# Seven half-products for eight in three pairs of pg and two of po, and ph to po in one planned order

## The chip, the cores and the metric

The kernel runs on 1 core of one Trainium2 chip. The metric is the device time of one execution in microseconds (us). The engines that matter are TensorE (PE; its weight loads are PEld), VectorE (DVE), ScalarE (ACT), GpSimd (POOL) and the DMA queue that SyncE (SP) issues.

## What is computed

An attention block and two feed-forward blocks, in float32:

```python
# q, k, v: (2, 12, 448, 64), causal attention in float32
scores = (q @ k.T) / 8, masked above the diagonal; attn = exp(scores - max); attn = attn / (sum + 1e-9)
x = (attn @ v) as (896 tokens, 768)
h = max(max(x @ w1, x @ w2), x @ w3)        # w1, w2, w3: (768, 768)
y = h @ wo                                  # (768, 768)
p = y @ w_in                                # (768, 2048)
g = where(p > 0, p, exp(min(p, 0)) - 1)
out = g @ w_out                             # (2048, 768)
```

The four weight matrices arrive as 64-bit floats; the kernel decodes their words into float32 itself.

## The kernel before

**Layout.** Everything is held transposed: features lie on the 128 partitions, tokens along the free dimension, 448 tokens for each of the two batches b. x, h and y are 6 chunks of 128 features for each b, g is 16. Each such tile is [128, 2, 448]: a high part that the fast matmul type (fp32r) holds exactly, and the rest, a low part. A weight block [128, n, 128] is split likewise into `hi` and `lo`. One product of a chunk is three matmuls of 448 columns: hi with high, hi with low, lo with high (`products`, L250, L251, L253).

**Stages.** Attention (12 head pairs), then ph (h: three matrices, 6 output blocks f, both b), py (y, 6 blocks), pg (16 blocks), po (6 blocks over 16 chunks, its weights in parts of 6, 5 and 5 chunks). A block of py or pg is 2 x 6 x 3 = 36 matmuls, a block of po 2 x 16 x 3 = 96.

**A weight's steps** (`less_steps` and `load_steps`): an SP transfer of 768 KB into one of two `w_raw` buffers, four steps on VectorE (L209, L212, L214, and after a ScalarE step at L216 the merge at L218), the high part on ScalarE (L236), the low part on VectorE (L224). There are two `w_raw`, two `w_f` and three pairs of hi/lo buffers.

**Seven products for eight in ph.** `unit(n, f1, f2)` computes two output blocks of one matrix for both b. It halves K (chunks 0 to 2 and 3 to 5), so that 2 batches x 2 halves x 2 blocks would be eight half-products of 3 chunks, 9 matmuls each, and it uses a scheme that needs seven. The price: sums of x over batches and halves, made once (`add_totals`, then `whole` splits each into high and low); two differences of weight blocks, "13" and "24" (`less_of`, L751), each split into high and low (`split`, L734, L224); three copies of a partial product into another PSUM bank, so that several results can go on from it (`seed`, L791), one product kept in SBUF (`out5`, L803) and added to two results (`both` in `leave`, L641). Five such units run, for blocks 1 to 4 of ph.

**Order.** Attention is ordered by one `Plan`, ph by a second one, `late_plan`: each task has engines with costs, tasks it comes after, buffers it takes and gives, and a rank; `order` picks greedily, and the result is each engine's program order (`manual_schedule`). TensorE's products are chained in one line (`on_pe`, 203 ns for each matmul). `late_plan` ends with the first two weights of py. py, pg and po are plain loops after it; there the order of each engine is that of the program text, and tiles are waited for as they are used.

**py, pg, po.** py's two results are split into y by ScalarE (L847) and VectorE (L156). pg's result goes through the ELU: two ScalarE steps (L862, L863), one VectorE step that joins (L866), a ScalarE high part (L868) and a VectorE low part (L156). po's results are copied out (L885) and stored. PSUM's eight banks go round.

Of the kernel before, what the change touches and what calls it, by code (L numbers as in the profile page):

```python
# [8 lines left out]
F32 = mybir.dt.float32  # L9
# [31 lines left out]
UNITS = ((1, 2), (3, 4))  # L41
FIRST = NK - 1
# [13 lines left out]
LOAD = (("DMA", 2300), ("DVE", 560), ("DVE", 356), ("DVE", 555), ("ACT", 937), ("DVE", 958))  # L56

# [75 lines left out]
def fused_kernel(ctx: ExitStack, tc: tile.TileContext, qk, v, w1, w2, w3, wo, wi2, wo2, outT):  # L133
# [7 lines left out]
    ident = const.tile([128, 128], F32, name="ident")  # L141
    make_identity(nc, ident)
    def causal(name, w, rows):

        m = const.tile([128, w], F32, name=name)
        nc.gpsimd.memset(m, 0.0)
        for at in range(0, 128, rows):
            own = m[at:at + rows, w - rows:]
            nc.gpsimd.affine_select(
                out=own, in_=own, compare_op=ALU.is_ge, fill=NEG, base=0, pattern=[[-1, rows]], channel_multiplier=1)  # L150
        return m

    mask, mask_r = causal("mask", FULL, C), causal("mask_r", S, R)

    def sub(eng, out, a, b):
        return eng.tensor_tensor(out=out, in0=a, in1=b.bitcast(F32), op=ALU.subtract)  # L156

    lift = const.tile([128, 1], F32, name="lift")
# [97 lines left out]
    y = [[None] * NK for _ in range(B)]  # L256

    with ExitStack() as s1:
        xp = s1.enter_context(tc.tile_pool(name="xp", bufs=2 * NK))
        bp = s1.enter_context(tc.tile_pool(name="bp", bufs=2))  # L260

        def keep_best(best, ps, n):
            if n == 0:
                nc.scalar.copy(best, ps)
            else:
                nc.vector.tensor_tensor(out=best, in0=ps, in1=best, op=ALU.max)

        AHEAD = [(f, n) for f in range(3) for n in range(3)][:AHEADS]
        tots = ExitStack()
        totp = tots.enter_context(tc.tile_pool(name="totp", bufs=4 * HALF, side="right"))  # L270
        totals = {(q, c): totp.tile([128, S], F32, tag="t", name=f"t{q}_{c}") for q in range(4) for c in range(HALF)}
        ahead, bests = {}, {}

        with ExitStack() as s2:
            raws = s2.enter_context(tc.tile_pool(name="raws", bufs=3))
            ap = s2.enter_context(tc.tile_pool(name="ap", bufs=PAIRS))
            thp = s2.enter_context(tc.tile_pool(name="thp", bufs=THS))
            small = s2.enter_context(tc.tile_pool(name="small", bufs=PAIRS))
            ps_s = s2.enter_context(tc.tile_pool(name="ps_s", bufs=SBANKS, space=PSUM))
            ps_t = s2.enter_context(tc.tile_pool(name="ps_t", bufs=6 - SBANKS, space=PSUM))  # L280
            plan = Plan(
                {"qk": QKS, "v": 3, "s": SBANKS, "pt": 6 - SBANKS, "m": 2, "pr": PAIRS, "th": THS, "raw": 2, "f": 2})
            engines = {"ACT": nc.scalar, "DVE": nc.vector, "POOL": nc.gpsimd}

            def copy(eng, out, a):
                (nc.scalar.copy if eng == "ACT" else engines[eng].tensor_copy)(out, a)

            ones, ones_row = (nc.const_aps.tensor(1.0, [128, w], BF16) for w in (128, 512))

            def warm(eng, n):  # L290

                idle = ps_m.tile([128, 512], F32, tag="m", name="idle")
                for _ in range(n):
                    nc.tensor.matmul(idle, ones, ones_row, start=True, stop=True)

            plan.add(warm, (8,), {"PE": 4200}, 0, takes=["m"], gives=["m"])

            SCORES = ((2, 0), (NB,), (1,))  # L300
            COLS = {(2, 0): 0, (2, 1): 1, (0, 0): 2, (0, 1): 3, (1, 0): 4, (1, 1): 5, (NB, None): 6}
            PARTS = ((0, 6), (6, 7))

            TURNS = (((0, 0, (0, 1, 2)),), ((1, 0, (0, 1, 2)),), ((0, 1, (1, 2)), (1, 1, (1, 2))),
                     ((0, 2, (2,)), (1, 2, (2,))), tuple((None, c, (NB,)) for c in range(NB + 1)))


            th_r = [thp.tile([C, 2, R], F32, name=f"th_r{n}", bufs=1) for n in range(THS)]
            for t in th_r:
                nc.gpsimd.memset(t, 0.0)  # L310

            us, xs_done, shares = {}, {}, []

            def heads(i):
                return (None,) if i == NB else (1, 0)

            def pair(p):

                u = us[p] = {}
                odd = p % 2  # L320

                def load(eng, part):
                    if "qk" not in u:
                        u["qk"] = raws.tile([128, 2, S], F32, tag="qk", name=f"qk{p}", bufs=QKS)
                    nc.sync.dma_start(u["qk"][:, :, part], qk[p][:, :, part])

                def load_v(eng):
                    u["v"] = raws.tile([C, 2, NB + 1, D], F32, tag="v", name=f"v{p}")
                    nc.sync.dma_start(u["v"], v[p])

                def scores(eng, g):

                    for e in (p, p + 1)[:1 + (g == 1)]:
                        us[e]["s", g] = [ps_s.tile([C, 512], F32, tag="s", name=f"s{e}_{g}_{j}") for j in range(2 - (g == 1))]
                    at = 0
                    for i in SCORES[g]:
                        w = min(C * (i + 1), S)
                        for e in (p, p + 1)[:1 + (i == NB)]:
                            for j in range(2):
                                own, to = slice(D * j, D * (j + 1)), j ^ (e % 2)  # L340
                                s = us[e]["s", g]
                                out = s[0][D * to:D * (to + 1), :w] if i == NB else s[j][:, at:at + w]
                                nc.tensor.matmul(  # L343
                                    out, us[e]["qk"][own, 0, C * i:w], us[e]["qk"][own, 1, :w], start=True, stop=True,
                                    skip_group_check=True)
                        at += w

                def least(eng, g, j):

                    if "nmx" not in u:  # L350
                        u["nmx"] = small.tile([C, len(COLS)], F32, tag="nmx", name=f"nmx{p}")
                        u["l"] = small.tile([C, len(COLS)], F32, tag="l", name=f"l{p}")
                    at = 0
                    for i in SCORES[g]:
                        w, n = min(C * (i + 1), S), COLS[i, j]
                        pr = u["pr", j, i] = ap.tile([C, w], F32, tag=f"pr{i}_{j}", name=f"pr{p}_{j}_{i}")
                        nc.vector.tensor_tensor_reduce(  # L357
                            out=pr, in0=u["s", g][j or 0][:, at:at + w],
                            in1=mask_r if i == NB else mask[:, FULL - w:], scale=-0.125, scalar=3.0e38,
                            op0=ALU.add, op1=ALU.min, accum_out=u["nmx"][:, n:n + 1],  # L360
                        )
                        at += w

                def exps(eng, g, j):
                    for i in SCORES[g]:
                        pr, n = u["pr", j, i], COLS[i, j]
                        nc.scalar.activation(  # L367
                            pr, pr, AF.Exp, bias=u["nmx"][:, n:n + 1], scale=-1.0, accum_out=u["l"][:, n:n + 1])

                def guard(eng, a, b):  # L370
                    engines[eng].tensor_scalar_add(u["l"][:, a:b], u["l"][:, a:b], 1e-9)

                def inverse(eng, a, b):
                    if "r" not in u:
                        u["r"] = small.tile([C, len(COLS)], F32, tag="r", name=f"r{p}")
                    nc.vector.reciprocal(u["r"][:, a:b], u["l"][:, a:b])  # L376

                def normalise(eng, i, j):
                    n = COLS[i, j]
                    engines[eng].tensor_scalar(  # L380
                        out=u["pr", j, i], in0=u["pr", j, i], scalar1=u["r"][:, n:n + 1], scalar2=1.0,
                        op0=ALU.mult, op1=ALU.mult)

                def turn(eng, t):
                    pt = u["pt", t] = ps_t.tile([128, 512], F32, tag="pt", name=f"pt{p}_{t}")
                    at = 0
                    for j, c, blocks in TURNS[t]:
# [5 lines left out]
                def turned(eng, t):  # L393

                    if "th" not in u:
                        u["th"] = thp.tile([C, NB, 2, S], F32, tag="th", name=f"th{p}")
                        u["th_r"] = th_r[p % THS]
# [529 lines left out]
```

## Time and profile before

| | |
|---|---|
| time, median of 3 runs | 483.97 us (482.69 to 485.89) |
| the profiled execution | 483.52 us, its span 481.70 us |
| TensorE busy | 474.9 us, 99% of the span, 2555 matmuls |
| VectorE busy | 351.8 us, 73%, 729 instructions |
| ScalarE busy | 254.6 us, 53%, 522 instructions |
| GpSimd busy | 47.7 us, 10% |
| transfers | 55.88 MB, mean 116 GB/s |
| mean granted TensorE clock | 0.999 |

A share of busy time is an average over stages; the stages begin at about 95 (ph alone), 204.67 (py), 247.87 (pg) and 363.07 us (po). Matmuls are pipelined, so one matmul's own duration (362 ns) is longer than the distance between two.

### The profile page before, as it was taken

What the parts mean: (1) busy time and instruction counts of PE and PEld (TensorE: products, weight loads), DVE (VectorE), ACT (ScalarE), POOL (GpSimd) and SP (SyncE); (2) the same over time, 40 slices, a digit from 0 to 9 for tenths busy, and PEclk for the clock granted to TensorE, in tenths of its full rate; (3) what the DMA queues carried; (4) which work ended last, traced back from release to release, by engine and by line L of the source; (5) the groups of instructions that cost most, each with busy time, mean ns of one, the idle gap of its engine ahead of it and who ended that gap; (6) DMA issues with size and microseconds to landing.
All of it is one profiled execution on the core that took longest, in us unless ns stands there. A gap on an engine that the chain in (4) does not pass through costs nothing.

```text
span 481.7 us, 6957 instructions
## 1 busy us (share of the span) xinstructions
PE 474.9 (99%) x2555; PEld 416.6 (86%) x2555; DVE 351.8 (73%) x729; ACT 254.6 (53%) x522; POOL 47.7 (10%) x101
## 2 busy tenths in 40 slices
PE   8999999999999999999999999999999999999997
PEld 3556666799999999999999999999999999999996
DVE  4999999699999999788767787687676544545310
ACT  5999796464464665455336666666664323322200
POOL 3575443500000000000000000000000000000000
PEclk9999999999999999999999999999999999999999
DMA  6626413013433333234433233233234434244011
GB/s 198 222 85 201 149 46 152 1 67 131 138 132 123 132 130 134 65 132 153 175 131 121 77 132 120 78 131 116 64 117 120 141 127 151 78 144 147 0 39 38
DMA packets 13969, 55.88 MB, mean 116 GB/s; under 512 B 1520, under 2 KB 3568, under 8 KB 13936
## 3 DMA queue, kind: packets, MB, share of 16 engines
q1 hardware_dynamic: 13936, 55.45, 33.9%
q8 instruction: 20, 0.33, 0.3%
q14 instruction: 13, 0.11, 0.1%
HBM read 52.69 MB, written 2.75 MB: 115 GB/s over the span
## 4 chain that ended last, share of the span: by engine, by line
PE 92%; DVE 4%; DMA 1%; POOL 1%; SPq 0%; issue 0%; ACT 0%; DVEq 0%; ACTq 0%
PE pg L251 8%; PE po L251 8%; PE po L253 8%; PE pg L253 8%; PE po L250 8%; PE pg L250 8%; PE p L778 7%; PE ps L778 6%; PE ph L250 4%; PE ph L251 4%; PE ph L253 4%; PE pt L390 4%; PE s L343 4%; PE o L413 3%; PE py L251 3%; PE py L253 3%
## 5 line engine op out<-in xcount | busy, mean ns | idle before, releaser
L251 PE MATMUL pg<-y,hi_wi 128*128 128x448 f32 x192 | 69.6, 362 | 0.0
L251 PE MATMUL po<-g,hi_wo 128*128 128x448 f32 x192 | 69.6, 362 | 0.0
L250 PE MATMUL po<-g,hi_wo 128*128 128x448 f32 x192 | 69.6, 362 | 0.0
L250 PE MATMUL pg<-y,hi_wi 128*128 128x448 f32 x192 | 69.6, 362 | 0.0
L253 PE MATMUL po<-g,lo_wo 128*128 128x448 f32 x192 | 54.8, 362 | 0.0
L253 PE MATMUL pg<-y,lo_wi 128*128 128x448 f32 x192 | 54.0, 362 | 0.0
L216 ACT ACTIVATE f_wo<-f_wo,lift 128x768 uint32<-128x768 int16 (+1 forms) x24 | 21.2, 886 | 43.4 <-DVE f_wo L214 43.3
L236 ACT ACTIVATE hi_wo<-f_wo 128x768 fp32r<-128x768 f32 (+1 forms) x24 | 19.0, 793 | 42.8 <-PE po L251 35.9
L224 DVE SCALAR_TENSOR_TENSOR lo_wo<-f_wo,hi_wo 128x768 fp32r<-128x768 f32 (+1 forms) x24 | 21.3, 891 | 26.6 <-ACT hi_wo L236 26.4
L367 ACT ACTIVATE pr<-pr,nmx 128x384 f32<-128x384 f32 (+1 forms) x72 | 35.9, 502 | 5.8 <-DVE nmx L357 5.7
L250 PEld LDWEIGHTS po<-g,hi_wo 128*128 128x128 f32 x192 | 36.0, 188 | 2.4
L253 PEld LDWEIGHTS po<-g,lo_wo 128*128 128x128 f32 x192 | 36.0, 188 | 2.4
L250 PEld LDWEIGHTS pg<-y,hi_wi 128*128 128x128 f32 x192 | 36.0, 188 | 2.4
L251 PEld LDWEIGHTS pg<-y,hi_wi 128*128 128x128 f32 x192 | 36.0, 188 | 2.4
L253 PEld LDWEIGHTS pg<-y,lo_wi 128*128 128x128 f32 x192 | 36.0, 188 | 2.4
L251 PEld LDWEIGHTS po<-g,hi_wo 128*128 128x128 f32 x192 | 36.0, 188 | 2.4
L250 PE MATMUL ph<-x,hi_w 128*128 128x448 f32 x96 | 35.3, 368 | 0.2 <-DVE x L156 0.2
L218 DVE SCALAR_TENSOR_TENSOR f_wo<-raw_wo,f_wo 128x768 int32<-128x768 int32 (+1 forms) x24 | 21.3, 891 | 19.4 <-ACT f_wo L216 19.3
L251 PE MATMUL ph<-x,hi_w 128*128 128x448 f32 x96 | 34.8, 363 | 0.0
L357 DVE CUSTOM_DVE_ANT_0 pr<-s,mask 128x384 f32<-128x384 f32 (+1 forms) x72 | 26.7, 414 | 7.0 <-PE s L343 6.9
L380 POOL TENSOR_SCALAR pr<-pr,r 128x384 f32<-128x384 f32 (+2 forms) x57 | 30.2, 548 | 12.1 <-DVE r L376 6.6
L253 PE MATMUL ph<-x,lo_w 128*128 128x448 f32 x96 | 30.0, 363 | 0.0
(143 smaller groups left out, 995.1 us busy)
## 6 DMA issues: line engine op xcount, KB each, us to landing
raw_w<-in_w SPq DMA_DIRECT2D x18, 768.0 KB, 4.6
raw_wi<-in_wi SPq DMA_DIRECT2D x16, 768.0 KB, 4.3
raw_wo<-in_wo SPq DMA_DIRECT2D x12, 768.0 KB, 4.5
raw_wo<-in_wo SPq DMA_DIRECT2D x12, 640.0 KB, 4.0
qk<-in_qk SPq DMA_DIRECT2D x11, 448.0 KB, 4.8
v<-in_v SPq DMA_DIRECT2D x12, 256.0 KB, 2.9
out_t<-ot SPq DMA_DIRECT2D x12, 224.0 KB, 3.0
qk<-in_qk SPq DMA_DIRECT2D x1, 256.0 KB, 3.2
```

Of the source, the lines that this page charges most:

```text
L216: nc.scalar.activation(f.bitcast(U32), y, AF.Relu, bias=lift, scale=2.0 ** 19)
L218: nc.vector.scalar_tensor_tensor(out=f, in0=below, scalar=13, in1=f, op0=ALU.logical_shift_right, op1=ALU.bitwise_or)
L224: nc.vector.scalar_tensor_tensor(out=lo, in0=f, scalar=-1.0, in1=hi.bitcast(F32), op0=ALU.mult, op1=ALU.subtract)
L250: nc.tensor.matmul(ps, hi[:, c, :], xs[cc][:, 0, :], start=(cc == 0), stop=False)
L251: nc.tensor.matmul(ps, hi[:, c, :], xs[cc][:, 1, :], start=False, stop=False)
L253: nc.tensor.matmul(ps, lo[:, c, :], xs[cc][:, 0, :], start=False, stop=(cc == total - 1))
L343: nc.tensor.matmul(out, us[e]["qk"][own, 0, C * i:w], us[e]["qk"][own, 1, :w], start=True, stop=True, skip_group_check=True)
L357: nc.vector.tensor_tensor_reduce(out=pr, in0=u["s", g][j or 0][:, at:at + w], in1=mask_r if i == NB else mask[:, FULL - w:], scale=-0.125, ...
L367: nc.scalar.activation(pr, pr, AF.Exp, bias=u["nmx"][:, n:n + 1], scale=-1.0, accum_out=u["l"][:, n:n + 1])
L380: engines[eng].tensor_scalar(out=u["pr", j, i], in0=u["pr", j, i], scalar1=u["r"][:, n:n + 1], scalar2=1.0, op0=ALU.mult, op1=ALU.mult)
L390: nc.tensor.transpose(pt[:e - C * c, at:at + C], u["pr", j if j is None else j ^ odd, i][:, C * c:e], ident)
L778: nc.tensor.matmul(ps[0], wt[:, HALF * k + c], w[:, i, :], start=(new and c == m == 0), stop=(c == HALF - 1 and m == 2), skip_group_check= ...
```

## The change

1. `unit` is made general (weights, left operand, sums and what becomes of the results are handed in) and gets a `lean` form with fewer buffers: one for both weights (`ub`), one for difference "13" (`u13`), two for the split differences (`ul`); difference "24" is formed in place over the weight buffer, once the first weight has been split.
2. pg computes blocks (2, 3), (6, 7) and (10, 11) by lean units over y. Their sums, `y_sums`, are formed from py's PSUM results, a chunk c as soon as blocks c and c + 3 are there; for that py goes through its blocks in the order 0, 3, 1, 4, 2, 5.
3. po computes blocks (2, 3) and (4, 5) by lean units for chunks 0 to 5 of g (768 of 2048 features); chunks 6 to 15 follow as two parts for each block, on the same banks. The sums over g, `sums_g`, are formed in the first blocks of po: eight VectorE steps a chunk, then four splits.
4. py, pg and po become tasks of `late_plan`, which now orders ph to po as one list; its SLACK goes from 200 to 110 and its overlap for VectorE from 70 to 60.
5. Tiles are reused by stage: y takes x's tiles, g those of h, then fresh ones, then those of the sums; the ELU's and the sums' intermediates use the `best` buffers of ph. The masks and `ident` move into the attention stage's pool, and POOL's small memset of `lift` comes before them. The size reserved for software DMA descriptors goes to 1024.

The core of the diff, without the re-indentation:

```diff
+PY = (0, 3, 1, 4, 2, 5)
+PG_UNITS = (2,6,10,)
+PO_UNITS = (2,4,)
...
-        late_plan.OVER = {"DVE": 70, "ACT": 60}
-        late_plan.SLACK = 200
+    late_plan.OVER = {"DVE": 60, "ACT": 60}
+    late_plan.SLACK = 110
...
-        def unit(n, f1, f2):
+    def unit(name, src, lean, left, sums, leave, kind="p"):
...
+        u, ut, tk = ("ub", "u13", "ul") if lean else ("u", "ut", "t")
...
+        if lean:
+            def less_in(at_, ab):
+                def sub_(eng):
+                    fs["24"] = slots(slice(1, 3)).rearrange("p s (c f) -> p (s c) f", c=HALF)
+                    a, b = ab()
+                    nc.vector.tensor_tensor(out=fs["24"][:, at_], in0=a, in1=b, op=ALU.subtract)
+                return sub_
+            t2 = task(less_in(dn, lambda: (fs[1][:, dn], fs["13"][:, up_])), "DVE", 555, at, [t1])
+            t4 = task(less_in(up_, lambda: (fs[0][:, dn], fs["24"][:, dn])), "DVE", 555, at, [t2, ready[0]])
...
+    renewed = task(again, "-", 0, clock[0] - 1000, [line[0], *left_last], gives=["ub", "u13", "ul", "ul", "ot", "ot"])
...
+    def y_sums(c, banks):
...
+        t0 = step("21", 0, (p21,), [e21], ["best0"], [m(1, c)], "ACT")
+        t1 = step("s0", 1, ("21", p22), [t0, e22], ["best1"], [m(1, d)])
+        t3 = step("s2", 2, (p11, "21"), [t0, e11], ["best0"], [], op=ALU.subtract)
+        t2 = step("s1", 3, ("s0", p11), [t1, t3], ["best1"], [m(0, c)], op=ALU.subtract)
...
+        for q, t, tag in ((0, t2, "best1"), (2, t3, "best0"), (1, t4, "best1"), (3, t4, "best0")):
+            sums_y.whole(q, c, lambda q=q: sy_home(HALF * q + c), lambda q=q: tot[f"s{q}"], at + 500,
+                         [t, renewed], gives=[tag])
...
+    for f in PY:
+        y_block(f, py_banks if PG_UNITS else None)
+        if f >= HALF and PG_UNITS:
+            y_sums(f - HALF, py_banks)
...
+        if f in PG_UNITS:
+            def leave_g(k, b, ps, after, gives, at, more=None, frees=()):
+                if more is not None:
+                    after = [*after, added(ps, more, after, at, frees)]
+                elu(f + k, b, ps, after, at, gives)
+            unit(f"g{f}", [wi2[f], wi2[f + 1]], True, y, sums_y, leave_g, "pg")
+            f += 2
+            continue
...
+        groups = ((0, 1, 3, 4), (2, 5)) if f == 0 else (tuple(range(NK)),)
...
+    sums_g, begin = Sums(), clock[0]
...
+            for k, (q, a, b_, op) in enumerate((
+                    (3, (1, c, 0), (1, c, 1), ALU.add), (0, 3, (1, d, 0), ALU.add), (0, 0, (1, d, 1), ALU.add),
+                    (1, (0, c, 0), (0, c, 1), ALU.add), (2, 1, 3, ALU.subtract), (1, 0, 1, ALU.subtract),
+                    (3, (0, d, 0), 1, ALU.subtract), (3, 3, (0, d, 1), ALU.add))):
...
+                t = task(step, "DVE", 619, at, [t, line[0], *(g_done[b, e] for b in range(B) for e in (c, d))],
+                         takes=[f"best{q % 2}"] * (k in (0, 1, 3, 4)))
...
+            unit(f"o{f}", [wo2[f, :, :NK], wo2[f + 1, :, :NK]], True, g, sums_g, leave_o, "po")
+        for c0, n in ((0, 6), (6, 5), (11, 5))[pair:]:
+            for k in reversed(range(1 + pair)):
+                single = f + pair == NK - 1 and c0 + n == NF and k == 0
+                for bs, t in o_parts(f + k, outs[k], c0, n, c0 == 0, single, sum((ends.get((k, b), []) for b in range(B)), [])):
...
+    with tc.manual_schedule():
+        for fn, eng, args in late_plan.order({"DVE": 1200, "ACT": 1000}):
+            fn(eng, *args)
```

## Rows read from the trace of the kernel before

**Rows 1.** Busy time by stage; columns: stretch, its length, engines, PEclk, DMA, GB/s.

```profile
0.00:95.00 95.00, 91.64 (x640) 57.17 (x641) 80.82 (x281) 73.29 (x235) 47.66 (x101) 1.00 0.38 134
204.67:247.87 43.20, 43.20 (x218) 40.55 (x217) 33.48 (x55) 19.94 (x29) 0.00 (x0) 1.00 0.41 148
247.87:363.07 115.20, 115.20 (x578) 108.14 (x577) 83.83 (x142) 72.61 (x125) 0.00 (x0) 1.00 0.32 106
363.07:478.30 115.23, 115.20 (x577) 107.80 (x575) 50.53 (x82) 29.10 (x41) 0.00 (x0) 1.00 0.32 101
```

**Rows 2.** The chain that ended last: start, us, what.

```profile
141.67 5.40 PE p L778 x27
...
478.35 0.53 ACT ot L885
```

**Rows 3.** VectorE by line and form in ph's units, 141.67 to 204.67 us.

```profile
L218 DVE SCALAR_TENSOR_TENSOR b<-raw_w,b 128x768 int32<-128x768 int32 x8 | 7.6, 955 | 1.1 <-ACT b L216 0.9
L224 DVE SCALAR_TENSOR_TENSOR lo<-f,hi 128x768 fp32r<-128x768 f32 x8 | 7.5, 951 | 0.0
...
L751 DVE TENSOR_TENSOR f<-b,f 128x384 f32<-128x384 f32 x8 | 4.5, 558 | 0.2
L214 DVE TENSOR_TENSOR b<-b 128x768 int16<-128x768 int16 x7 | 3.9, 558 | 0.2
L751 DVE TENSOR_TENSOR f<-b 128x768 f32<-128x768 f32 x4 | 3.8, 958 | 0.1
...
L209 DVE TENSOR_SCALAR b<-raw_w 128x768 bf16<-128x768 bf16 x6 | 3.3, 554 | 0.0
...
L212 DVE TENSOR_SCALAR b<-b 128x768 int16<-128x768 int16 x7 | 2.5, 360 | 0.2
L641 DVE TENSOR_TENSOR p<-p,s 128x448 f32<-128x448 f32 x4 | 2.5, 628 | 0.1
...
L224 DVE SCALAR_TENSOR_TENSOR lo<-b,hi 128x384 fp32r<-128x384 f32 x4 | 2.2, 551 | 0.0
```

**Rows 4.** VectorE by line and form in pg, 247.87 to 363.07 us.

```profile
L156 DVE TENSOR_TENSOR g<-gf,g 128x448 fp32r<-128x448 f32 x30 | 17.3, 619 | 0.0
L866 DVE SCALAR_TENSOR_TENSOR gf<-e,pg 128x448 f32<-128x448 f32 x30 | 17.2, 614 | 0.0
L224 DVE SCALAR_TENSOR_TENSOR lo_wi<-f_wi,hi_wi 128x768 fp32r<-128x768 f32 x14 | 13.4, 958 | 13.1 <-ACT hi_wi L236 13.1
```

**Rows 5.** Busy time: two units of ph, two blocks of pg, two of po.

```profile
141.67:154.27 12.60, 12.60 (x65) 11.83 (x64) 11.93 (x19) 6.73 (x12) 0.00 (x0) 1.00 0.38 125
...
179.47:192.07 12.60, 12.60 (x65) 11.83 (x64) 12.18 (x21) 7.18 (x11) 0.00 (x0) 1.00 0.38 133
...
247.87:255.07 7.20, 7.20 (x38) 6.76 (x37) 4.37 (x7) 2.64 (x5) 0.00 (x0) 1.00 0.28 104
255.07:262.27 7.20, 7.20 (x38) 6.76 (x37) 5.35 (x9) 4.69 (x9) 0.00 (x0) 1.00 0.32 107
363.07:382.27 19.20, 19.20 (x98) 18.02 (x97) 11.51 (x20) 7.83 (x13) 0.00 (x0) 1.00 0.40 114
382.27:401.47 19.20, 19.20 (x98) 18.02 (x97) 9.90 (x17) 5.36 (x8) 0.00 (x0) 1.00 0.41 133
```

**Rows 6.** VectorE in order of time: start, us, what.

```profile
167.25 0.62 DVE L266 TENSOR_TENSOR best<-ps,best 128x448 f32<-128x448 f32 x1
167.79 0.61 DVE L156 TENSOR_TENSOR h<-best,h 128x448 fp32r<-128x448 f32 x1
```

**Rows 7.** VectorE in order of time, at the end of pg's second block.

```profile
261.02 0.96 DVE L218 SCALAR_TENSOR_TENSOR f_wi<-raw_wi,f_wi 128x768 int32<-128x768 int32 x1 [1.01 <-ACT f_wi L216]
```

**Rows 8.** ScalarE's copies between banks in ph's units, by line.

```profile
L791 ACT COPY ps<-p 128x448 f32<-128x448 f32 x15 | 7.8, 517 | 12.4 <-PE p L778 12.3
```

**Rows 9.** Who waited for whom in pg: us in total, times, longest.

```profile
ACT hi_wi L236 <- PE pg L251: 12.9, 13, 1.8
```

**Rows 10.** POOL in order of time: its first task behind the masks.

```profile
9.75 0.24 POOL L371 TENSOR_SCALAR l<-l 128x6 f32<-128x6 f32 x1 [6.56 <-ACT pr L367]
```

More of the change, by code (lines that the diff above doesn't have):

```diff
@@ L139, in fused_kernel @@
     ps_m = ctx.enter_context(tc.tile_pool(name="ps_m", bufs=2, space=PSUM))
[L141 to L153, printed above, removed]
     def sub(eng, out, a, b):
         return eng.tensor_tensor(out=out, in0=a, in1=b.bitcast(F32), op=ALU.subtract)
+    const.tile([128, 64], F32, name="place")
     lift = const.tile([128, 1], F32, name="lift")
@@ new lines, in fused_kernel, with on_pe, task, convert @@
+    clock, line = [0.0], [None]
+    PASS = 203.0
+    def on_pe(fn, n, after, **more):
+        t = late_plan.add(fn, (), {"PE": int(PASS * n)}, 0, [*after, line[0]], lead=clock[0], **more)
+        clock[0] += PASS * n
+        line[0] = t
+        return t
+    def task(fn, eng, cost, at, after, **more):
+        return late_plan.add(fn, (), {eng: cost}, 0, after, lead=at, **more)
+    LAST, LAST_5 = (("ACT", 848), ("DVE", 958)), (("ACT", 735), ("DVE", 825))
+    def convert(steps, costs, at, took, gave, begun=False):
+        got, t = [], None
+        def step(eng):
+            got[:] = [next(steps)]
+        for k, (eng, cost) in list(enumerate(costs))[begun:]:
+            t = task(step, eng, cost, at, [t], takes=took.get(k, ()), gives=gave.get(k, ()))
+        return got, t
@@ new lines, in finish, with high, low, standard @@
+    def finish(f, b, at, after):
+        def high(eng):
+            nc.scalar.copy(h[b][f][:, 0], best_of(f, b))
+        def low(eng):
+            sub(nc.vector, h[b][f][:, 1], best_of(f, b), h[b][f][:, 0])
+        t = task(high, "ACT", 570, at, [after])
+        hs_done[f, b] = task(low, "DVE", 617, at, [t], gives=[f"best{b}"])
+    def standard(n, f, over):
+        at, ps = clock[0], {b: [] for b in over}
+        parts, t = (([ahead[f, n]], None) if (f, n) in AHEAD else load(
+            (w1, w2, w3)[n][f], f"w{n}_{f}", at, begun.pop(n, None) if f == FIRST else None))
+        def product(eng):
+            for b in over:
+                ps[b].append(psum(f"ph{n}_{b}_{f}"))
+            products([ps[b][0] for b in over], *parts[0], [x[b] for b in over], 0, NK, NK)
+        t = on_pe(product, 18 * len(over), [t], takes=["m"] * len(over), gives=["w"])
+        for b in over:
+            leave(n, f, b, ps[b], [t], ["m"], clock[0] + 2000)
@@ new lines, in fused_kernel, with __init__, whole, high @@
+    class Sums:
+        def __init__(self):
+            self.parts, self.made = {}, {}
+        def whole(self, q, c, home, total, at, after, gives=()):
+            def high(eng):
+                self.parts[q, c] = home()
+                nc.scalar.copy(self.parts[q, c][:, 0], total())
+            def low(eng):
+                sub(nc.vector, self.parts[q, c][:, 1], total(), self.parts[q, c][:, 0])
+            t = task(high, "ACT", 570, at, after)
+            self.made[q, c] = task(low, "DVE", 617, at, [t], gives=gives)
@@ L637, in leave, with put, out @@
+    def put(f, b, ps, after, at, eng, gives, more=None, frees=()):
+        def out(eng_):
+            ot = pools["ot"].tile([128, S], F32, tag="ot", name=f"ot{f}_{b}")
+            rows = outT[128 * f:128 * (f + 1), S * b:S * (b + 1)]
             if more is not None:
[L639 to L645 removed]
@@ L830, in fused_kernel @@
-        opened = task(reopen, "-", 0, 0, list(made.values()))
-        for fs_ in UNITS:
-            for n in range(1 if fs_ == UNITS[0] else 0, 3):
-                unit(n, *fs_)
-        wos = [load(wo[f], f"wo_{f}", clock[0] + 7300 * f)[0] for f in range(2)]
-        with tc.manual_schedule():
-            for fn, eng, args in late_plan.order({"DVE": 1200, "ACT": 1000}):
-                fn(eng, *args)
-        up.close()
-        ctx.enter_context(tc.tile_pool(name="pad", bufs=1, side="right")).tile([128, 24], F32, name="pad")
@@ L871, in fused_kernel @@
[L871 to L886 removed]
+                nc.vector.tensor_tensor(out=ot, in0=ps[0], in1=more[0], op=ALU.add)
+            else:
+                (nc.scalar.copy if eng == "ACT" else nc.vector.tensor_copy)(ot, ps[0])
```

1077 lines of the change are left out of this document (592 added, 485 removed).

## The prediction

> **What bounds the kernel now.** I read the busy times by stage first. TensorE is busy for all of the 43.20 us of py, the 115.20 us of pg and the 115.20 us of po; the only idle time worth a name is 3.36 us in the attention stage (95.00 less 91.64) and the 3.40 us between the end of po at 478.30 and the end of the span at 481.70 [rows 1]. In the chain of waits the second half of the span is nothing but matmuls, 27 of them in 5.40 us, which is 0.200 us each, then one copy and the last transfer [rows 2]. pg gives the same price: 115.20 us for 16 x 36 = 576 matmuls (the window's 578 counts two that straddle an edge). The granted clock is full in every stage. So from ph's middle on the time is a count of matmuls, each 0.200 us, and there is no gap at ph/py, py/pg or pg/po for a list-scheduled order to close: handing tiles on by stage can gain nothing, it can only keep a new wait from arising. Second I read VectorE by line and by stage, because every matmul that the change removes is paid for in VectorE and ScalarE steps.
>
> The profiled execution is 483.52 us, its span 481.70 us; the median of the runs is 483.97 us, 0.45 above it. I subtract from the median.
>
> **TensorE: what is removed.** `unit` issues 7 products of 9 matmuls, 63, where two blocks of pg take 72. Three pairs of pg save 27. A pair of po does the same for 6 of its 16 chunks of K: again 9 each, 18 for two pairs. 45 x 0.200 = **9.00 us** off a path that has no other idle time. Nothing is added on TensorE; py's and pg's first blocks only take their chunks in another order.
>
> **VectorE: what is added.** A pair needs, by the rows of ph's units, two weights decoded (0.554 + 0.360 + 0.558 + 0.955 = 2.43 each), three differences (0.958 + 2 x 0.558 = 2.07), four low parts (3 x 0.951 + 0.551 = 3.40), two additions of the kept product (2 x 0.628 = 1.26) [rows 3], and four times the ELU's two steps, 0.614 + 0.619 [rows 4]: 16.5 us by durations, in 25 instructions. A plain block is 2.43 + 0.96 + 2 x 1.23 = 5.85 us in 9 instructions, yet VectorE is busy only 5.35 us in such a block of 7.20 us [rows 5]: neighbours overlap, two of 0.62 us start 0.54 us apart [rows 6], 0.055 us an instruction on average. So a pair costs 16.5 - 25 x 0.055 = 15.1 us against its 12.60 us of TensorE, a sum step 0.62 - 0.055 = 0.565 us, a plain weight 3.39 - 5 x 0.055 = 3.1 us. The pair alone is more than VectorE can do in its time; with two plain blocks behind it, it is 25.8 of 27.0 us. Four budgets follow, VectorE's work against TensorE's time:
>
> Up to the first pair's third product (61.2 us from 204.67). Before, VectorE was busy 33.48 us in py [rows 1] and 4.37 + 5.35 us in the first two blocks of pg [rows 5]: 43.2. Of this 8.4 us went into weights for f = 2, 3 and 4 (two whole, and the fourth step of the third just done [rows 7]), which need not be ready by then. Added: three chunks of `y_sums`, each 4 steps and 4 low parts on VectorE, 24 x 0.565 = 13.6 us, and the pair's own preparation up to its third operand, 4.85 + 2.07 + 2.85 less 14 overlaps = 9.0 us. Sum 57.4 of 61.2 us: it fits, with 3.8 us to spare.
>
> Blocks 2 to 11: 3 x 15.1 + 4 x 5.35 = 66.7 against 3 x 12.6 + 4 x 7.2 = 66.6 us. VectorE is full, and lives on the 3.8 us.
>
> Blocks 12 to 15: 21.4 of 28.8 us; what is late is caught up.
>
> po up to the first pair's sixth product (47.4 us): 11.51 + 9.90 [rows 5], less 9.7 us of weights made for later parts, plus `sums_g` (3 chunks of 8 steps and 4 low parts, 36 x 0.565 = 20.3), plus 9.0 + 0.5 for the pair: 41.5 us. It fits with 5.9 us to spare. The sums wait for the last matmul of pg, so none of this can be done earlier; the third and fourth sums (a third of the steps) are needed only by the fifth and sixth product.
>
> **ScalarE** has per pair three copies of a partial product into another bank and one into SBUF (0.52 each [rows 8]) and one and a half more high parts, at most 1.5 us by the longest ScalarE step, L216, for which VectorE waits 1.01 us [rows 7]: 9.1 + 2.1 + 1.5 = 12.7 us in 12.6, 21.8 of 27.0 with two plain blocks (72.61 / 16 = 4.54 a block [rows 1]). Each copy has the 1.8 us of the product in between as its cover; without it TensorE waits for the rest of a step in front of it (1.01 us at most) and the copy, so a few tenths at worst per copy. ph's units run the same copies and TensorE never waits there.
>
> **What I cost at nothing.** The weight loads move into the planned order of SP's queue, with the output transfers between them: two weights in 12.6 us is what ph's units already load with the transfers a third busy [rows 5], and a queued load delayed by an output copy is covered by weights that stand ready: they wait for TensorE to free their buffers, 13 times, 12.9 us in sum [rows 9]. If that cover is gone, one late load costs at most the 7.2 us in which a block of pg loads one weight, once. The masks and `ident` are made one small memset later on POOL: it then sits idle 6.56 us before its next task [rows 10], which is the cover. New addresses: no row tells; I take zero, and 0.5 us either way for the range. PSUM: a pair opens five banks, as in ph, and ELU frees one by its second step; with eight banks ELU may lag by about a block, which is a little more slack for blocks 2 to 11. The tail is one copy and one transfer, as before.
>
> **The sum:** 483.97 - 9.00 = 474.97, and some 0.5 us for waits of tenths at five pairs, where VectorE has nearly no slack: **475.5 us**.
>
> **Where a rule of the skill speaks against it.** Of two neighbouring VectorE steps the second starts 0.08 us before the first has ended [rows 6]. The Trainium skill, page "VectorE: DVE Perf Modes", section "The DRAIN you can't avoid", says that the next operation does not start until the pipe is empty, and that chaining does not avoid it. The trace disagrees for this kernel's steps; by that rule a pair would cost the full 16.5 us, and it is a rival below.
>
> **Rivals.** (1) VectorE reaches only the share that it reached in ph's units, 11.93 and 12.18 of 12.60 us, some 95% [rows 5]. Then the first budget leaves 0.8 us, blocks 2 to 11 need 70.2 us, 2.8 us more than there is: 477.8 us; with the lean pairs' single buffers it may be some 2 us more. For it: dependent steps and ScalarE's answers leave gaps that no order fills. Against it: TensorE never waited in those units, so 95% may have been all that was wanted there. I give it 0.25, and 476.5 to 481.
>
> (2) Slower than before: the lean pair's third operand is formed in place, behind the first operand's low part, which needs a free hi/lo buffer. If the planned order lets a later plain block take that buffer, the chain from its release is three VectorE steps, 0.95 + 0.56 + 0.95 [rows 3], and two on ScalarE of at most 1.01 each, 4.5 us, plus one or two foreign steps (0.9 us) ahead of each of the three, 5 to 9 us, against the 3.6 us after which the third product is due. Up to 5 us per pair: from 1.8 us on a pair loses more than its nine matmuls, and at 3.6 us, five pairs cost 18 us: 493 us. Against it: the buffer is freed 7.2 us before the pair begins if the loads stay in order. 0.08.
>
> (3) No overlap on VectorE. Blocks 2 to 11 need 3 x 16.5 + 4 x 5.85 = 72.9 us, 6.3 too many, the first budget 57.4 x 5.85 / 5.35 = 62.8, 1.6 too many: 474.97 + 7.9 = 482.9 us, no change. 0.05, since rows 6 speak against it. This is the page's rule.
>
> (4) The matmuls don't fall to 2510: then 484 us or more. 0.02.
>
> **How the numbers follow.** 0.60 for the forecast (474 to 477), then the rivals as given. Within 1% (479.1 to 488.8) is about what a measurement of this kernel can tell from no change. Faster by over 1%: 0.60 plus the better part of rival 1, 0.14: 0.74. Slower by over 1%: rival 2, 0.07. Within 1%: 0.19. The runs of before spread from 482.69 to 485.89, so the low end is 482.69 - 9.00 = 473.7. The high end takes in rival 1, 481.0; rivals 2 and 3 (and 4) stay outside.
>
> **What the profile after would show.** 2510 matmuls, and the span 9.0 us shorter if TensorE stays at 0.200 us with no idle from 95 us on. VectorE over 95% busy from py's middle to block 11, falling to some 75% in blocks 12 to 15, then near 90% up to po's first pair. If I am wrong by rival 1, TensorE waits on `lo` parts or sums at the second and third pair of pg; by rival 2, it waits on operand "24" at all five. An attention stage longer than 95 us would show a cost of the new addresses that I have not counted.

## The result, and the profile after

The changed kernel takes 476.01 us (median of 6 runs, 474.95 to 476.45) against 483.97 for the kernel before on the same chip: a ratio of 0.9828, 95% interval 0.9805 to 0.9851, faster by 1.7%. The forecast was 475.5 us in 473.7 to 481.0. The profiled execution took 476.45 us, its span is 474.7. (Some medians below include one or two executions more than 1.5% longer than the fastest of the same kernel; the ratio beside them leaves these out and is the number to read.)

The page of the changed kernel, its head:

```profile
span 474.7 us, 6946 instructions
...
PE 465.0 (98%) x2510; PEld 407.5 (86%) x2510; DVE 403.6 (85%) x822; ACT 282.0 (59%) x577; POOL 47.2 (10%) x101
```

45 matmuls fewer, as announced; VectorE has 51.8 us more work, ScalarE 27.4.

Busy time by stage, changed kernel (columns as in [rows 1]): py; pg's blocks 0 and 1; blocks 2 to 11 with the three pairs; 12 to 15; po up to its first pair; the rest of po.

```profile
206.65:249.85 43.20, 43.20 (x217) 40.54 (x217) 40.65 (x70) 23.39 (x38) 0.00 (x0) 1.00 0.35 123
249.85:264.25 14.40, 14.40 (x73) 13.51 (x73) 14.09 (x24) 8.30 (x17) 0.00 (x0) 1.00 0.20 76
264.25:330.85 66.60, 66.60 (x334) 62.50 (x334) 61.51 (x104) 54.27 (x95) 0.00 (x0) 1.00 0.33 119
330.85:359.65 28.80, 28.80 (x145) 27.03 (x145) 24.95 (x44) 19.89 (x36) 0.00 (x0) 1.00 0.35 107
359.65:398.05 38.40, 38.40 (x193) 36.04 (x193) 37.22 (x64) 18.61 (x30) 0.00 (x0) 1.00 0.37 118
398.05:471.30 73.25, 73.19 (x366) 68.30 (x365) 39.58 (x68) 22.90 (x35) 0.00 (x0) 1.00 0.32 104
```

The second and the third figure of each line are the length and TensorE's busy time: they are the same to 0.06 us, so nothing new holds TensorE from py on in this execution. pg takes 109.80 us for [rows 1]'s 115.20, 27 matmuls of 0.200 less. The fifth figure (VectorE) shows who pays.

The chain of the changed kernel, its first transfer and the first ph unit (start, us, what):

```profile
2.07 6.69 DMA qk<-in_qk
...
143.65 5.40 PE p L805 x27
```

In [rows 2] that unit begins at 141.67. From the unit's start to the end of the span it is 481.7 - 141.67 = 340.03 us before and 474.7 - 143.65 = 331.05 after: 8.98 less, the 9.00 of the sum. But the two spans differ by 7.0 us only: the unit starts 1.98 us later. What TensorE waits for shows where (us in total, times, longest):

```profile
PE s L347 <- DMA qk<-in_qk: 2.9, 2, 1.7
PE ph L241 <- DVE x L146: 1.2, 1, 1.2
```

In the trace of before these two are 1.0 and 0.2 us, and the transfer is 0.92 us shorter:

```profile
2.07 5.77 DMA qk<-in_qk
```

```profile
PE s L343 <- DMA qk<-in_qk: 1.0, 1, 1.0
PE ph L250 <- DVE x L156: 0.2, 1, 0.2
```

So the question for the experiments: does the change cost 2 us in the attention stage, which it hardly touches?

### The profile page after: what moved, and what is told of

It reads as the page before. It is cut to its first block, busy times and chain, and to the rows that moved or that the text cites. A ratio compares the mean times of both kernels' runs of the same rounds, so it can differ in the third digit from the quotient of the medians.

```text
span 474.7 us, 6946 instructions
## 1 busy us (share of the span) xinstructions
PE 465.0 (98%) x2510; PEld 407.5 (86%) x2510; DVE 403.6 (85%) x822; ACT 282.0 (59%) x577; POOL 47.2 (10%) x101
## 4 chain that ended last, share of the span: by engine, by line
PE 91%; DVE 5%; DMA 1%; POOL 1%; SPq 0%; issue 0%; ACT 0%; DVEq 0%
PE pg L911 10%; PE p L805 8%; PE py L911 6%; PE ps L805 6%; PE po L911 5%; PE pg L915 5%; PE ph L241 4%; PE ph L242 4%; PE ph L244 4%; PE pt L394 4%; PE s L347 4%; PE o L417 3%; PE pg00g L805 3%; PE py L915 3%; PE po L915 3%; PE po00o L805 2%
## 5 line engine op out<-in xcount | busy, mean ns | idle before, releaser
L911 PE MATMUL pg<-x,hi_wi 128*128 128x448 f32 x240 | 57.7, 362 | 0.0
L911 PEld LDWEIGHTS pg<-x,hi_wi 128*128 128x128 f32 x240 | 45.0, 188 | 3.0
L911 PE MATMUL py<-h,hi_wo 128*128 128x448 f32 x144 | 34.6, 362 | 0.0
L915 PE MATMUL pg<-x,lo_wi 128*128 128x448 f32 x120 | 33.7, 362 | 0.0
L347 PE MATMUL s<-qk 64*128 64x256 f32 (+3 forms) x192 | 27.0, 443 | 3.4 <-DMA qk<-in_qk 2.9
L207 ACT ACTIVATE f_wo<-f_wo,lift 128x640 uint32<-128x640 int16 (+1 forms) x20 | 17.4, 874 | 19.6 <-DVE f_wo L205 19.5
L911 PEld LDWEIGHTS py<-h,hi_wo 128*128 128x128 f32 x144 | 27.0, 188 | 1.8
L290 ACT COPY th<-pt 128x384 f32<-128x384 f32 (+2 forms) x42 | 19.4, 483 | 11.7 <-PE pt L394 11.2
L417 PE MATMUL o<-th,v 128*64 128x448 f32 (+2 forms) x144 | 24.4, 448 | 0.1
L915 PEld LDWEIGHTS pg<-x,lo_wi 128*128 128x128 f32 x120 | 22.5, 188 | 1.5
L394 PE MATMUL pt<-ident,pr 128*128 128x128 f32 x144 | 22.4, 283 | 0.8 <-POOL pr L384 0.6
L209 DVE SCALAR_TENSOR_TENSOR f_wo<-raw_wo,f_wo 128x640 int32<-128x640 int32 (+1 forms) x20 | 17.3, 875 | 3.9 <-ACT f_wo L207 3.9
```

Source lines behind the costliest of these rows:

```text
L347: nc.tensor.matmul(out, us[e]["qk"][own, 0, C * i:w], us[e]["qk"][own, 1, :w], start=True, stop=True, skip_group_check=True)
L394: nc.tensor.transpose(pt[:e - C * c, at:at + C], u["pr", j if j is None else j ^ odd, i][:, C * c:e], ident)
L417: nc.tensor.matmul(u["o"][D * j:D * (j + 1), C * c:], u["v"][:, j, c], u["th_r"][:, j ^ odd] if c == NB else u["th"][:, c, j ^ odd, C * c: ...
L911: nc.tensor.matmul(p[0], hi[:, c, :], xs[j][c0 + c][:, i, :], start=first and c == 0 and i == 0, stop=False, skip_group_check=True)
L915: nc.tensor.matmul(p[0], lo[:, c, :], xs[j][c0 + c][:, 0, :], start=False, stop=last and c == n - 1, skip_group_check=True)
```

## The experiments

**The changed kernel again**, for a second profile.

> The changed kernel once more, for a second profile. In its first profile TensorE's first ph unit starts 1.98 us later than before, and from there to the last matmul everything is exactly 9.00 us shorter. Theory A (the 1.98 us are two chances of the attention stage: the landing of the second pair's qk, 8.76 against 7.84 us, and a VectorE sum step beside a GpSimd one that took 1.58 for 0.62 us just ahead of a step that TensorE waits for): this profile shows other values in at least one of the two places, a span between 472.7 and 474.7, and the span from the first ph unit on the same to 0.1 us. Theory B (the new addresses and the new start of GpSimd cost 2 us in every run): both places as in the first profile to 0.1 us, span 474.6 to 474.8. Time 475 to 476.5 under both.

476.39 us, ratio 0.9841 (0.9821 to 0.9861). The transfer of the second pair's queries and keys took 5.35 us this time, not 6.69, so that part of the delay is not the program's; the wait of 1.2 us for x_lo (the low part of x, the second of the two waits above) was there again. From the first ph unit to the end of the span it took 474.6 - 142.38 = 332.22 us, 1.17 more than in the first profile, where I had expected the same to 0.1 us: a wait stood in po's second pair that the first profile does not have (TensorE in order of time):

```profile
441.49 0.68 PE L805 MATMUL po00o<-x,hi_o 128*128 128x448 f32 x2 [0.81 <-ACT pos1o L818]
```

**The attention side alone**: before, with the masks and `ident` in the attention stage's pool, a tile in their old place, and the smaller descriptor memory. No pairs, plain loops.

```diff
-    mask, mask_r = causal("mask", FULL, C), causal("mask_r", S, R)
+    const.tile([128, 64], F32, name="place")
...
+            mask, mask_r = causal("mask", FULL, C), causal("mask_r", S, R)
...
-    nc = bacc.Bacc("TRN2", target_bir_lowering=False, num_devices=1)
+    nc = bacc.Bacc("TRN2", target_bir_lowering=False, num_devices=1, dynamic_dma_scratch_size=1024)
```

> The kernel before with only the attention side of the change: masks and ident in the attention stage's pool, the small memset of GpSimd ahead of them, the 64-float tile, 1024 for the descriptors; no pairs, no planned order behind ph. Theory A (chance): within 0.3% of the kernel before, 483 to 485 us, the first ph unit starting anywhere from 141.7 to 143.7 us. Theory B (addresses and start): 1 to 2 us slower than before, 485 to 486 us, the first ph unit at 143.6 us as in the changed kernel.

484.07 us, ratio 1.0005 (0.9994 to 1.0017). No cost that can be measured (at most 0.8 us by the interval), though its profile has the wait of 1.2 us for x_lo; the transfer took 4.91 us there.

**The list order alone**: no pairs.

```diff
-PG_UNITS = (2,6,10,)
-PO_UNITS = (2,4,)
+PG_UNITS = ()
+PO_UNITS = ()
```

> The changed kernel without its five pairs: py, pg and po in the planned order, but all products plain (2555 matmuls). Theory A: the order alone gains nothing, since TensorE had no gap to close: 483 to 485 us, no TensorE idle time between 145 us and the last matmul. Rival (the order by itself costs or gains at the stage borders): TensorE idle time at 208, 251 or 366 us, and a time more than 1.5 us off the kernel before.

484.56 us, ratio 1.001 (0.9997 to 1.0023), no idle time of TensorE from the first ph unit to the last matmul. The planned order of py, pg and po and the tiles handed on by stage neither gain nor cost: all of the gain is the pairs'.

**The kernel before again**, unchanged, for a second profile.

> The kernel before, unchanged, for a second profile. If what delays the first ph unit in the changed kernel comes from its added instructions, VectorE's sum step at the attention's end takes 0.62 us here as in the first profile and the first ph unit starts at about 141.7 us; if it is chance which of VectorE and GpSimd starts first, it may take 1.58 us here, with GpSimd's steps shorter, and x_lo 1.0 us later. The landing of the second pair's queries and keys, 5.77 us after issue in the first profile, shows how far that varies with the same program.

484.52 us, one execution. The wait of 1.2 us for x_lo is in this profile too, and the first unit starts at 142.69. It was the first profile of before that was the exception: of the ten profiles here without the exchange of additions that follows below, nine have the stretched step. VectorE, then GpSimd, in order of time, in the first profile of before:

```profile
84.79 0.62 DVE L549 TENSOR_TENSOR t<-x 128x448 f32<-128x448 f32 x1
85.33 0.62 DVE L156 TENSOR_TENSOR x<-o,x 128x448 fp32r<-128x448 f32 x1
...
84.82 3.08 POOL L549 TENSOR_TENSOR t<-t,x 128x448 f32<-128x448 f32 x2 [5.02 <-ACT x L286]
```

and in its second:

```profile
84.83 1.58 DVE L549 TENSOR_TENSOR t<-x 128x448 f32<-128x448 f32 x1
86.33 0.61 DVE L156 TENSOR_TENSOR x<-o,x 128x448 fp32r<-128x448 f32 x1
...
84.80 1.13 POOL L549 TENSOR_TENSOR t<-t,x 128x448 f32<-128x448 f32 x1 [4.96 <-ACT x L286]
```

The same program; in one execution VectorE is 0.03 us ahead and its sum step takes 0.62 us, in the other GpSimd is 0.03 us ahead and the step takes 1.58, and x_lo behind it starts 1.0 us later. The Trainium skill, page "SBUF — State Buffer", section "SBUF: two separate sides", has the rule: a VectorE operation with two inputs in SBUF and a GpSimd operation that reads SBUF want the same port pair, and whichever starts first keeps it for its whole instruction. The rows agree: VectorE's step ends at 86.41, 0.48 us after GpSimd's first step at 85.93, where it takes 0.62 us when nothing holds it.

With this the start of the first ph unit is accounted for in eight profiles, to about 0.1 us: it is 136.0 us plus the time of that one transfer, and 1.0 more where the step is stretched.

| profile | transfer, us | stretched | first unit, us |
|---|---|---|---|
| before | 5.77 | no | 141.67 |
| before again | 5.79 | yes | 142.69 |
| after | 6.69 | yes | 143.65 |
| after again | 5.35 | yes | 142.38 |
| attention side alone | 4.91 | yes | 141.88 |
| list order alone | 5.55 | yes | 142.53 |
| before, lower pieces first (below) | 6.20 | no | 142.11 |
| lower pieces first, step held (below) | 5.49 | no | 141.58 |

None of the 1.98 us has to be the change's. (Two more, pairs in pg alone and the dearer transfer, start 0.6 and 0.9 us later than this rule; both had a granted clock of 0.94 in the first 30 us, the others 1.00. In the remaining four the chain does not begin with that transfer, so they do not test the rule.)

**The lower pieces first**: an edit of the changed kernel in the attention's sums, so that GpSimd's step waits for x_lo and can't run beside the sum step.

```diff
-                    (t1, t4, h22, ALU.add), (t1, t1, l22, ALU.add),
+                    (t1, t4, l22, ALU.add), (t1, t1, h22, ALU.add),
```

> The changed kernel with two additions of the sums over x exchanged, so that GpSimd's first sum step reads the low part of x and so comes after VectorE's step that makes it (the same sums, added in another order). Theory A: the VectorE step that TensorE waits for no longer stands behind a stretched one: it ends some 1.0 us earlier than in the first profile of the changed kernel, the ph products of that place start 0.6 us or less after the ScalarE step before them plus one VectorE step, and the time is up to 1 us below the changed kernel's, 474.5 to 475.5. Rival (the stretched step is not GpSimd's doing): the same 1.5 us step stands there again and the time is 476.0.

475.16 us, ratio 0.9814 (0.9795 to 0.9832), an interval that overlaps with those of the changed kernel; and in the trace the sum step is back at 0.62 us:

```profile
84.17 0.62 DVE L553 TENSOR_TENSOR t<-x 128x448 f32<-128x448 f32 x1
84.71 0.62 DVE L146 TENSOR_TENSOR x<-o,x 128x448 fp32r<-128x448 f32 x1
...
85.41 2.95 POOL L553 TENSOR_TENSOR t<-t,x 128x448 f32<-128x448 f32 x2 [6.24 <-DVE x L146]
```

**The same edit in the kernel before**, alone.

> The kernel before with one edit alone: in the sums at the attention's end, which VectorE and GpSimd form, the lower piece of x is added before the higher one, so that GpSimd's step waits for x_lo and VectorE's sum step has no GpSimd step beside it. No pairs, the matmuls as before. Theory (the stretched sum step is chance in the kernel before as well, in most executions, and costs 1.0 us whenever it happens): x_lo is never late, the first ph unit starts at about 141 us, and the time is 483.0 to 483.5 us, a ratio of 0.998. Rival (the stretch belongs to the changed kernel in the main, and the low pieces first gain nothing here): a ratio of 1.000.

483.2 us against 483.39, ratio 0.9997 (0.9985 to 1.001). The stretch is gone in the profile, but the time is not measurably better. So the edit is worth at most some 0.7 us here, and the theory as I wrote it (1.0 us in most executions, ratio 0.998) is not borne out; how often the stretch occurs outside of profiles stays open.

**po's wait.** The order of ScalarE in the changed kernel's second profile:

```profile
437.12 0.54 ACT L832 COPY s_o<-po130o 128x448 f32<-128x448 f32 x1 [1.28 <-PE po130o L805]
440.18 0.83 ACT L207 ACTIVATE f_wo<-f_wo,lift 128x640 uint32<-128x640 int16 x1 [2.53 <-DVE f_wo L205]
440.92 0.53 ACT L818 COPY pos1o<-po00o 128x448 f32<-128x448 f32 x1
```

and of VectorE, ahead of it:

```profile
433.01 0.82 DVE L209 SCALAR_TENSOR_TENSOR f_wo<-raw_wo,f_wo 128x640 int32<-128x640 int32 x1
...
438.70 0.50 DVE L200 TENSOR_SCALAR f_wo<-raw_wo 128x640 bf16<-128x640 bf16 x1 [2.56 <-DMA raw_wo<-in_wo]
```

Read backwards: the copy `pos1o`, for which TensorE waits, has its input since 438.9 but stands in ScalarE's queue behind the decode step L207 of a later weight, which waits for VectorE's L205, which waits for a transfer, which was issued at 433.86, when the merge L209 had freed its raw buffer. Two edits test this. First, the planner's cost of a weight's transfer, 1.92 us for these (2.30 for the larger ones), set to 4.6 us, so that it would put such steps later (with the lower pieces first):

```diff
+LANDING = 4600
...
+            cost = LANDING if eng == "DMA" else cost
```

> The kernel with the exchanged additions, and the planner of ph to po told 4.6 us for a weight's transfer in place of 2.3 and 1.92 (the traces show 4.1 to 4.9 from issue to landing). Theory C (in po's second pair ScalarE stands in front of its third copy with the decode step of a later weight, whose transfer the planner thought landed 2.5 us earlier, and TensorE waits 0.6 to 0.8 us): with the true cost that decode step comes behind the copy, TensorE has no idle time from the first ph unit to the last matmul, and the time is 0.6 us below that of the exchanged additions, about 474.5. Rival (VectorE alone is late there, whatever the order): the same 0.6 us of TensorE idle time at the second pair, same time, 475.2.

479.75 us, ratio 0.9893 (0.9876 to 0.9910): that wait is gone, but the whole list is ordered anew, and TensorE waits 3.7 us elsewhere for high and low parts. This is no fair test of a truer cost: to the cost of a transfer the planner adds a lag of 2.0 us (`LAG`), so it had reckoned with 3.9 us from issue to landing and now reckons with 6.6, where such transfers take 4.1 us in the median of the changed kernel's profile (4.8 for the one read here). Second, one edge alone: L207 of those weights comes after the copy (with the lower pieces first).

```diff
-            t = task(step, eng, cost, at, [t], takes=took.get(k, ()), gives=gave.get(k, ()))
+            t = task(step, eng, cost, at, [t, *(behind if k == 4 else ())], takes=took.get(k, ()), gives=gave.get(k, ()))
...
+        parts, t = load(wo2[f, :, c0:c0 + n], f"wo2_{f}_{c0}", clock[0], n=n, behind=seeds[-1:] if c0 == 11 and f >= PO_UNITS[-1] else ())
```

> The changed kernel with the lower pieces of the attention's sum first (as in e4_low_first) and, in po, ScalarE's decode step of the weights whose load lands late put behind the copy of the second pair's second operand (pos1o). Theory (the decode step stands in ScalarE's queue until its transfer has landed, and the copy stands behind it): the wait of TensorE for pos1o, 0.6 us in e4_low_first, is gone, no other wait in its place, and the time is 474.5 us, a ratio of 0.980. Rival (the copy is late because VectorE is full there, not because of the queue): the wait stays or becomes one for the decoded weights, and the time is 475.2 or more.

Ratio 0.9811 (0.9797 to 0.9826), the profiled execution 474.39 us with a span of 472.6. No wait is there from the first ph unit on, and the copy now runs as soon as its input is there; ScalarE:

```profile
438.03 0.52 ACT L820 COPY pos1o<-po00o 128x448 f32<-128x448 f32 x1 [1.26 <-PE po00o L807]
438.46 0.83 ACT L207 ACTIVATE f_wo<-f_wo,lift 128x640 uint32<-128x640 int16 x1
```

The rival, that VectorE is full there, falls: VectorE's load from 425 to 435 us is the same as with the lower pieces first alone (9.19 and 9.14 us of 10), only the place in the queue has changed, and the copy starts 0.04 us after its input is there instead of 2.3. That TensorE's wait went with it is not shown by this one profile: the transfer landed early in it (VectorE waited 2.09 us for it, 2.59 with the lower pieces first alone), as in the first profile of the changed kernel (2.04), where the copy was 0.9 us late and TensorE did not wait. This is the lowest ratio of all, but it cannot be told from the 0.9814 without the hold, and against the changed kernel itself the intervals overlap too.

**Which pairs pay.** Pairs in pg alone (`PO_UNITS = ()`), then in po alone (`PG_UNITS = ()`).

> The changed kernel with its three pairs in pg and none in po: 27 matmuls fewer than before. If the gain is the matmul count alone: 484.2 - 5.4 = 478.8 us, no TensorE idle time from the first ph unit on. Rival (the pairs in pg lose something of it to waits): above 479.5 us, with TensorE idle time at blocks 2, 6 or 10.

> Pairs in po alone, none in pg; the rest as in the changed kernel. 2537 matmuls, 18 fewer than before. Theory (po's pairs are paid for at 0.200 us a matmul, and are free beside the rest): 484.2 - 3.6 = 480.6 us, less at most 0.8 us for one wait on the second pair's second operand; ratio 0.992 to 0.994. Rival (po's pairs cost what they save in waits, and pg's alone give the gain): 483 us or more.

pg alone: ratio 0.9883 (0.9861 to 0.9905), a gain of 5.7 us where the count gives 5.4, and no wait of TensorE from the first ph unit on. po alone: 481.76 us, ratio 0.9953 (0.9941 to 0.9966), 2.3 us where the count gives 3.6; its profile has the wait for `pos1o` (0.4 us) again. Together 8.0 us, as measured for both at once (8.3 and 7.7 by the two ratios).

**A fourth pair in pg.** `PG_UNITS = (2,4,7,10)`: the first two stand side by side, and one plain block lies ahead of each of the others, where the changed kernel has two.

> The changed kernel with four pairs in pg, at blocks 2, 4, 7 and 10. 9 more matmuls fall, 1.8 us. VectorE's work from 206.65 to the end of block 11 was 116.3 of 124.2 us in the changed kernel; a fourth pair adds some 15.1 - 10.7 = 4.4 us and takes 1.8 us of time: 120.7 of 122.4. If VectorE's total is the limit, it still fits: no TensorE idle time in pg, 474.2 us. If the single buffers of the lean pairs or VectorE's order set the limit (rival 2 of the prediction, or rival 1), TensorE waits at the pairs that stand next to each other, 2 us or more, and the time is 476 or above.

479.1 us, ratio 0.9883 (0.9864 to 0.9901): 9 matmuls fewer and 2 to 3 us slower than with three. TensorE waits:

```profile
PE pg00g L805 <- ACT hi_g L746: 1.6, 3, 0.6
PE pg00g L805 <- DVE lo_g L215: 1.3, 3, 0.6
```

```profile
280.00 0.68 PE L805 MATMUL pg00g<-s,hi_g 128*128 128x448 f32 x2 [0.62 <-ACT hi_g L746]
281.06 0.47 PE L805 MATMUL pg00g<-s,lo_g 128*128 128x448 f32 x1 [0.38 <-DVE lo_g L215]
```

and VectorE is full in the 10 us ahead of the first of these waits (9.91 of 10):

```profile
270.00:280.00 10.00, 9.38 (x48) 8.46 (x47) 9.91 (x18) 9.34 (x19) 0.00 (x0) 1.00 0.43 157
```

The product at 280.00 is the third of the second pair: its operand is "24". The third product of the third and of the fourth pair waits in the same way, at 301.25 and 322.43, and VectorE is as full ahead of these (10.19 of 10.30 us from 291.00, 10.40 of 10.50 from 312.00). Its total is not the limit, 117.97 us of 125.42 from py to the end of block 11; it is full just where an operand is due.

**po's pairs one block earlier.** `PO_UNITS = (1, 3)`, so that 19.2 us fewer lie between pg's end and the first pair.

> The changed kernel with po's two pairs at blocks 1 and 3, one block (19.2 us) earlier. The number of matmuls stays. If VectorE's budget ahead of po's first pair is as worked out (sums over g 20.3 us and the pair's preparation 9.5, none of which can start ahead of pg's last matmul, and some 5 us for the last ELU and block 0), it needs 35 us where TensorE gives 28.2: TensorE waits some 7 us at the first pair, 483 us. If the sums are not what is late, no TensorE idle time and 476 us.

492.07 us, ratio 1.0156 (1.0124 to 1.0188): slower than before. TensorE waits 12.7 us for the sums over g, all of it in the second product of the first pair, where I had expected some 7. Decode steps of later weights stand between the sums in VectorE's order. The windows show what an idle TensorE costs besides:

```profile
PE po130o L805 <- DVE x L146: 6.4, 2, 3.5
PE po130o L805 <- ACT x L699: 6.3, 2, 5.1
```

```profile
380.00:390.00 10.00, 1.34 (x4) 0.65 (x4) 9.79 (x18) 4.19 (x8) 0.00 (x0) 0.73 0.23 66
390.00:400.00 10.00, 6.54 (x21) 5.52 (x22) 7.41 (x14) 3.36 (x6) 0.00 (x0) 0.59 0.33 93
400.00:410.00 10.00, 10.00 (x52) 9.38 (x51) 6.14 (x11) 3.60 (x5) 0.00 (x0) 1.00 0.50 156
```

## Why the prediction was right, and where it was not

**TensorE's term** is right to the hundredth: 2510 matmuls, and 8.98 us between first unit and end where 9.00 was said (7.81 in the second profile, which has po's wait). That list order and handed-on tiles gain nothing is shown by the run without pairs.

**The 0.5 us allowance** is of the right order and in the wrong place, so that the time came within 0.5 us of the forecast is in part luck. It stood for waits of tenths at all five pairs, for want of VectorE. No profile of the changed kernel has one at pg's pairs. What there is, is a wait at po's second pair, 0.8 us in the second profile, and it comes from a step that I costed at nothing: "a queued load delayed by an output copy is covered by weights that stand ready". The weight itself is so covered; but its decode step is in ScalarE's queue ahead of a copy that is due. I asked who waits for the late weight, and not what is queued behind the step that waits for it. Nor did I make a budget for the stretch between po's two pairs, where VectorE is 9.64 of 10 us busy before that transfer can start (425 to 435 us). In the first profile of after the same sequence ends in time, because TensorE came there 1.2 us later while the transfer landed at the same time to 0.1 us.

**VectorE's second budget** was wrong: "VectorE is full, and lives on the 3.8 us" counts the first pair's preparation, 9.0 us, in the first budget and again among 3 x 15.1. Corrected, py to block 11 needs 57.4 + 66.7 - 9.0 = 115.1 of 124.2 us; measured 40.65 + 14.09 + 61.51 = 116.25. The sum so corrected is right to 1% (up to the first pair's third product 57.78 us measured, 57.4 said), and the slack was 8 us rather than none. So the signs that I gave are off as well: 92% in py's second half (19.92 of 21.60 us), 98 and 92% behind it, where over 95% was said throughout, 87% in blocks 12 to 15 (24.95 of 28.80, said some 75%), 97% before po's first pair (said near 90%). The work is spread later than I had put it. The fourth budget, the sums over g, holds for the work that was due: up to the first pair's sixth product VectorE was busy 45.60 of 47.40 us, but from 401.70 on (4.7 us) with parts of weights that TensorE takes only from 410.49 on, which leaves some 41 where 41.5 was said. One block earlier TensorE waited 12.7 us where the same working gave some 7, with decode steps of later weights between the sums: the order spends such a slack before it is needed.

**The step that nothing need be paid at the new addresses** holds: the attention stage was longer in the profile, the sign that I had named for such a cost, but the stretched step stands in the second profile of before too, the transfer differs by 1.34 us between two profiles of the changed kernel, and the attention side alone costs nothing that can be measured. One detail was wrong without effect: the ELU frees a bank of PSUM with its third step (the join reads it), not with its second; no matmul waited for a bank in either profile.

**Rival 1** (VectorE stops at 95%): 9.91 and 9.79 of 10 us where TensorE waited for it speak against that; so 95% is not all that VectorE can reach. **Rival 2** did not occur with three pairs, but its mechanism is real: with four pairs closer together it is operand "24" that comes late, by tenths and not the 5 us that I had put at the worst. **Rival 3**, the page "VectorE: DVE Perf Modes" of the Trainium skill, section "The DRAIN you can't avoid": by it py to block 11 would need 115.1 x 5.85 / 5.35 = 125.9 us of 124.2; VectorE did the work in 116.25, with independent steps 0.54 us apart. That section itself allows that a next operation which isn't held starts earlier, which is what these rows show. **Rival 4** is out with the count.

Open: why the changed kernel's two ratios (0.9828 and 0.9841) lie 0.7 and 1.3 us above what 9.00 alone would give (0.9814, which the first interval includes and the second does not). po's wait with its restart (below) is 0.9 us in the second profile and is of that size; that it is there in most executions isn't shown.

## What to carry to other kernels

Where one engine has no idle time, taking work from it pays by the count, as long as the engine that pays in its place has slack in each stretch between two due times: make one budget for each, every task in one alone, and leave none out. For each late transfer ask not only who needs the data, but what is queued behind the first step that waits for it. And before a microsecond in a profile is put down to an edit, profile the unedited kernel twice.

## What the runs showed of the hardware

- A VectorE step with both inputs in SBUF (0.62 us alone) took 1.56 to 1.58 us when a GpSimd step on SBUF had started 0.03 to 0.06 us earlier; GpSimd's step then took 1.13. Where VectorE's had started 0.03 us earlier, it took 0.62, and GpSimd's first two steps together 3.08. Which it is differs between executions of one program.
- A TensorE that has waited loses a little more than the wait: behind the 0.81 us, the two matmuls from 441.49 were followed by the third at 442.00, 0.51 us after the first one's start where two take 0.40 otherwise. It was so behind the wait of 0.64 us in the run with the lower pieces first too (439.88 to 440.39); the granted clock was 1.00 in both.
- In the run with po's pairs earlier the granted clock fell to a mean of 0.73 and 0.59 in the two stretches of 10 us in which TensorE stood idle for most or a third of the time, so towards the lower of its two levels (1.2 of 2.4 GHz), and was back at 1.00 in the next: 12.7 us of waits cost some 16 us against the changed kernel.
